# Second layer's first product by Strassen's seven products, with Mish as one activation

## The chip, the cores and the metric

One NeuronCore of a Trainium2 chip runs the whole program. The metric is the device time of one execution in microseconds (us); less is better. Times come from timed runs of the program and from one profiled execution of it, whose trace lists every instruction of every engine: PE (matrix products; PEld is its loading of stationary operands), ACT (activations and copies), DVE (elementwise work), POOL, and SP, which here only issues transfers.

## The reference, cut to what matters

Local attention (4 batches, 8 heads, 768 positions, head width 64) gives x with 3072 rows and 512 columns. Two dense layers follow:

```
h = x @ w_in                                     # 3072x512 by 512x2048
g = maximum(h, 0) + alpha * minimum(h, 0)        # layer 1
x = g @ w_out                                    # 3072x2048 by 2048x512
h = x @ w_in2                                    # layer 2, same shapes
g = h * tanh(log(1 + exp(h)))                    # "Mish" (log1p(exp) replaced by h above 20)
out = g @ w_out2
```

All of it is float32. The weights come as 64-bit floats and are turned into 32-bit ones on the chip.

## The kernel before, in words

**Products.** Every float32 operand of a large product is split into a high part (a cast, `h`) and a low remainder (`l`), and a product is the sum of three: high*high, high*low, low*high. So a product of a 128x128 stationary tile with a moving tile of n columns is three matmuls.

**Tiling.** Rows of x come in 6 blocks of 512 (`BN`). The 2048 inner features come in 16 units of 128 (index j). For a block and a unit, `gemm1` (line 884) forms the unit's h for 512 rows in one PSUM bank: 4 steps over the 512 input features times three, 12 matmuls of 512 columns (all of them the call at L897). The first two units of the first block alone are done in halves of 256 rows, in 48 matmuls of 256 columns, because half the rows are ready earlier. Then comes the nonlinearity, then `split_g` (high by ACT, L909, low by DVE, L910) and `gemm2` (line 941): 12 matmuls of 512 columns (L961) that add the unit's share into four PSUM banks, one for each 128 rows of output (layer 2) or 128 output features (layer 1). After 16 units `evac` (line 969) copies the four banks out.

**Layer 2's nonlinearity** is `act2` (line 924): for a unit three activations on ACT (Exp, Ln, Exp) and six instructions on DVE (L929 to L936).

**Banks and buffers.** Banks 0 to 3 collect the second products, banks 4 to 7 hold h. The split g lives in two slots; x of a block in two alternating buffers. Layer 1's result goes through DRAM (`yd`); `load_y` (line 986) reads a block of it back and splits it, four 512-wide casts and four subtractions.

**Weights.** Layer 1's weights stay in 32 buffers of SBUF (`wi0..15`, `wo0..15`). Layer 2's are converted during layer 1 and put in DRAM (`spill_w`, line 338, in blocks 2 to 4), and come back into the 32 buffers during the last block of layer 1 as those come free (`reload_w`, line 344). They stay for all of layer 2.

**Order of the work.** Each piece of work is a task given to `Plan` (line 69) with its engine, an assumed duration, what it reads and what it writes. `Plan.run` works out due times backwards and then lays the tasks out engine by engine; each engine executes its list in that order, and an instruction that has to wait holds back all behind it on its engine. PE's order is that of the main loop (line 1050): gemm1 of a unit, then gemm2 of the unit `LAG` before it (2 in layer 1, 4 in layer 2). Attention work for later blocks is woven into layer 1.

Of the kernel before, what the change touches and what calls it, by code (L numbers as in the profile page):

```python
# [21 lines left out]
E20 = 485165195.40979028  # L22
# [152 lines left out]
def chunked_attention_moe_moe_kernel(  # L175
# [82 lines left out]
    two = cp.tile([P, 1], F32, name="two")  # L258
# [4 lines left out]
    nc.gpsimd.memset(two, 2.0)  # L263
# [17 lines left out]
    w2f = {}  # L281
# [56 lines left out]
    def spill_w(item, at):  # L338
        f = to_f32(item, load_raw(item, at=at), at=at)
        d = Buf(lambda: dp.tile([P, 512], F32, name=f"w2f{item[1]}{item[2]}"))  # L340
        add("sp", dma_(P * 2048), lambda: nc.sync.dma_start(d.t, f.t.bitcast(F32)), [f], [d], at=at)
        w2f[item] = d

    def reload_w(item):
        f, d = wfs.next(), w2f.pop(item)
        add("sp", dma_(P * 2048), lambda: nc.sync.dma_start(f.t.bitcast(F32), d.t), [d], [f])
        split_w(item, f)
# [516 lines left out]
    def open_second():  # L864


        def open_():
            if "bp" not in phase:
                att_pools.close()
                phase["bp"] = ctx.enter_context(tc.tile_pool(name="bp", bufs=1))  # L870

        second["raw"] = raw2.next()
        for tag, n in (("u", 3), ("n", 2), ("rc", 2), ("e", 2), ("o", 3)):
            shape = [P, BN]

            def make(tag, shape):
                open_()
                return phase["bp"].tile(shape, F32, tag=tag, name=tag)

            second[tag] = Ring([lambda t=f"{tag}{i}", s=shape: make(t, s) for i in range(n)], att_bufs)  # L880
# [43 lines left out]
    def act2(blk, j, h, n_):  # L924
        u, n, r, e = (second[t].next() for t in ("u", "n", "rc", "e"))
        v = nc.vector
        hs = lambda: h.t[:, :BN]
        add("act", a_(BN) - 0.05, lambda: nc.scalar.activation(u.t, hs(), AF.Exp), [h], [u])  # L928
        add("dve", d_(BN, True), lambda: v.tensor_scalar_min(u.t, u.t, E20), [], [u])  # L929
        add("dve", d_(BN), lambda: v.scalar_tensor_tensor(n.t, u.t, 2.0, u.t, ALU.add, ALU.mult), [u], [n])  # L930
        add("act", a_(BN) + 0.09, lambda: nc.scalar.activation(e.t, n.t, AF.Ln, bias=two[:, 0:1]), [n], [e])  # L931
        add("act", a_(BN), lambda: nc.scalar.activation(r.t, e.t, AF.Exp, scale=-1.0), [e], [r])  # L932
        add("dve", d_(BN), lambda: v.scalar_tensor_tensor(e.t, n.t, 2.0, r.t, ALU.add, ALU.mult), [n, r], [e])  # L933
        add("dve", d_(BN), lambda: v.scalar_tensor_tensor(r.t, e.t, 2.0, r.t, ALU.subtract, ALU.mult), [e], [r])  # L934
        add("dve", d_(BN), lambda: v.tensor_mul(n.t, n.t, r.t), [r], [n])
        add("dve", d_(BN), lambda: v.scalar_tensor_tensor(u.t, n.t, -1.0, hs(), ALU.mult, ALU.mult), [n, h], [u])  # L936
        uu = Buf(lambda: [u.t])
        uu.uses = u.uses
        split_g(1, blk, j, uu, BN)

    def gemm2(layer, blk, j):
# [7 lines left out]
        for a in range(na):  # L949
            bk = accs[layer, blk][a]  # L950
            n = BLOCKS[blk][1] if layer == 0 else DM

            def go(a=a, bk=bk, n=n):
                cs = slice(a * P, (a + 1) * P)
                (gh, gl), (wh, wl) = g.t, (w.t[:, z, :] for z in range(2))
                if layer == 0:
                    prods = [(wh[:, cs], gh), (wh[:, cs], gl), (wl[:, cs], gh)]
                else:
                    prods = [(gh[:, cs], wh), (gh[:, cs], wl), (gl[:, cs], wh)]
                for i, (lt, rh) in enumerate(prods):  # L960
                    nc.tensor.matmul(bk.t[:, :n], lt, rh, start=j == 0 and i == 0, stop=j == NJ - 1 and i == 2)  # L961

            add("pe", 3 * p_(n), go, [w, g], [bk])
            if j == NJ - 1:
                evac(layer, blk, a, bk)

    yds = {}

    def evac(layer, blk, a, bk):
# [6 lines left out]
        else:  # L976
            o = rstrip.next(DM) if a == 0 else second["o"].next()

            def view():
                return o.t[0] if a == 0 else o.t  # L980

            row = blk * BN + a * P
            add(BOTH, a_(DM), lambda e: copy_on(e, view(), bk.t), [bk], [o])
            add("sp", dma_(P * DM * 4), lambda: nc.sync.dma_start(out[row : row + P, :], view()), [o])

    def load_y(blk):
        t0 = blk * BN
        frm = [b for i, b in yds.items() if BLOCKS[i][0] < t0 + BN and t0 < sum(BLOCKS[i])]
        (x, views, _, _), = parts = new_x(BN)
        raw = second["raw"]  # L990
        for kk in range(KT):
            key = raw, kk % 2

            def xr(kk=kk):
                return raw.t[:, kk % 2 * BN : (kk % 2 + 1) * BN]

            def high(xr=xr, kk=kk):
                nc.scalar.copy(views()[0][:, kk, :], xr())

            def low(xr=xr, kk=kk):  # L1000
                xh, xl = (t[:, kk, :] for t in views())
                nc.vector.tensor_sub(xl, xr(), xh.bitcast(F32))

            def load(xr=xr, kk=kk):
                nc.sync.dma_start(xr(), yd[:, kk, t0 : t0 + BN])

            add("sp", dma_(P * BN * 4), load, [(b, kk) for b in frm], [key])
            add("act", a_(BN), high, [key], [(x, ("h", kk))])
            add("dve", d_(BN), low, [key, (x, ("h", kk))], [(x, ("l", kk))])
        return parts  # L1010


# [3 lines left out]
    w2_items = [(1, side, j) for j in range(NJ) for side in "io"]  # L1016
# [23 lines left out]
    W2B = 2  # L1040
    LAG = (2, 4)
    tiles = [(layer, blk, j) for layer in range(2) for blk in range((NBA, NB)[layer]) for j in range(NJ)]
    pend = []
    xcur = xts[0]
    xnext = None

# [3 lines left out]
    for layer, blk, j in tiles:  # L1050
# [8 lines left out]
        if j == 0:  # L1059
            if (layer, blk) == (0, NBA - 1):  # L1060
                open_second()
            xcur = xts.pop(blk) if layer == 0 else xnext
        n = BN if layer else BLOCKS[blk][1]
        h = early[j] if (layer, blk) == (0, 0) and j < SPLIT else gemm1(layer, blk, j, xcur, n)
        if layer == 0:
            i = ((blk - W2B) * NJ + j) * 32 // ((NBA - 1 - W2B) * NJ)
            if blk < NBA - 1 and 0 <= i < len(w2_items) and w2_items[i] not in w2f:
                spill_w(w2_items[i], plan.now)
            elif blk == NBA - 1 and j == 0:
                xnext = load_y(0)  # L1070
        elif j == 2 and blk + 1 < NB:
            xnext = load_y(blk + 1)
        weave(2 * j)
        (act1 if layer == 0 else act2)(blk, j, h, n)
        pend.append((layer, blk, j))
        while len(pend) > LAG[layer]:
            t2 = pend.pop(0)
            gemm2(*t2)
            if t2[:2] == (0, NBA - 1):
                for side in "io":  # L1080
                    reload_w((1, side, t2[2]))
        weave(2 * j + 1)
    while pend:
        gemm2(*pend.pop(0))
# [58 lines left out]
```

## Time and profile before

| | |
|---|---|
| timed runs, 3 | 1117.82 to 1118.26 us, median 1118.02 us |
| profiled execution: span from first to last instruction | 1116.8 us |
| PE busy in the span | 1109.0 us (99%) |
| PEld, DVE, ACT busy | 914.6 (82%), 789.2 (71%), 580.4 us (52%) |
| HBM read and written | 74.85 and 20.97 MB |

The span is 1.2 us shorter than the median of the timed runs; the profile lists no other time of its execution. A matmul's duration in the trace is longer than the distance to the next one, since matmuls overlap: the pace is read from the distance of starts. The same holds of PEld's loads.

### The profile page before, as it was taken

How to read it: one execution, taken by the hardware profiler on the slowest of the kernel's cores; microseconds unless marked ns; L12 is line 12 of the kernel's file. 1: busy time of each engine (PE TensorE's matmuls, PEld its weight loads, DVE VectorE, ACT ScalarE, POOL GpSimd, SP SyncE). 2: the span in 40 equal slices, each digit the busy share in tenths (PEclk: the TensorE clock that was granted, in tenths of full speed). 3: DMA queues.
4: the chain of work that ended last, by engine and by line, in shares of the span. 5: the costliest groups of instructions: out<-in, count | busy, mean ns of one | idle time of the engine just before them, and what ended most of it. 6: DMA issues, size and time to landing. Idle time of an engine off the chain costs nothing.

```text
span 1116.8 us, 19091 instructions
## 1 busy us (share of the span) xinstructions
PE 1109.0 (99%) x7566; PEld 914.6 (82%) x7571; DVE 789.2 (71%) x1378; ACT 580.4 (52%) x1267; POOL 6.6 (1%) x20
## 2 busy tenths in 40 slices
PE   8999999999999999999999999999999999999998
PEld 5888888888888888888888888888888888888887
DVE  6898546476575756645459788778778878777775
ACT  6888434455454554545456445445446445444543
POOL 2000000000000000000000000000000000000000
PEclk9999999999999999999999999999999999999999
DMA  9976211345454455334332001002002000100101
GB/s 279 309 210 179 89 32 50 106 160 177 123 172 134 131 175 150 98 116 133 95 95 95 1 16 61 1 1 76 1 1 76 1 1 20 38 1 1 38 0 38
DMA packets 56585, 97.05 MB, mean 87 GB/s; under 512 B 5296, under 2 KB 24240, under 8 KB 56496
## 3 DMA queue, kind: packets, MB, share of 16 engines
q1 hardware_dynamic: 56496, 95.84, 28.3%
q8 instruction: 59, 0.97, 0.4%
q14 instruction: 30, 0.25, 0.1%
HBM read 74.85 MB, written 20.97 MB: 86 GB/s over the span
## 4 chain that ended last, share of the span: by engine, by line
PE 99%; DMA 1%; SPq 0%; issue 0%; DVE 0%; ACT 0%
PE bank L897 47%; PE bank L961 47%; PE bank L715 2%; PE bank L649 1%; PE bank L1023 1%; DMA wo<-in_kw_dram 1%; PE bank L593 0%; PE bank L762 0%; PE bank L526 0%; PE bank L786 0%; SPq L425 0%; SPq L418 0%; DVE wo L551 0%; ACT o L251 0%; DVE st L574 0%
## 5 line engine op out<-in xcount | busy, mean ns | idle before, releaser
L897 PE MATMUL bank<-xh,wi 128*128 128x512 f32 (+1 forms) x1552 | 506.6, 388 | 0.0
L897 PEld LDWEIGHTS bank<-xh,wi 128*128 128x128 f32 x1552 | 290.4, 188 | 59.9
L897 PE MATMUL bank<-xl,wi 128*128 128x512 f32 (+1 forms) x776 | 300.2, 387 | 0.0
L961 PE MATMUL bank<-gh,wo 128*128 128x512 f32 x768 | 253.3, 391 | 0.0
L961 PE MATMUL bank<-wo,gh 128*128 128x512 f32 x768 | 236.4, 389 | 0.0
L897 PEld LDWEIGHTS bank<-xl,wi 128*128 128x128 f32 x776 | 145.7, 188 | 29.4
L961 PEld LDWEIGHTS bank<-gh,wo 128*128 128x128 f32 x768 | 144.2, 188 | 30.3
L961 PEld LDWEIGHTS bank<-wo,gh 128*128 128x128 f32 x768 | 144.2, 188 | 30.0
L961 PE MATMUL bank<-gl,wo 128*128 128x512 f32 x384 | 149.5, 389 | 0.0
L961 PE MATMUL bank<-wo,gl 128*128 128x512 f32 x384 | 149.4, 389 | 0.0
L919 DVE SCALAR_TENSOR_TENSOR rstrip<-rstrip,nalpha 128x512 f32<-128x512 f32 x96 | 72.0, 750 | 107.0 <-ACT rstrip L916 106.4
L909 ACT CAST gh<-u 128x512 fp32r<-128x512 f32 x96 | 59.8, 623 | 156.3 <-PE bank L961 156.2
L915 ACT ACTIVATE rstrip<-bank 128x512 f32<-128x512 f32 x96 | 57.9, 604 | 110.8 <-PE bank L897 107.5
L910 DVE TENSOR_TENSOR gl<-rstrip,gh 128x512 fp32r<-128x512 f32 x96 | 66.2, 690 | 62.3 <-ACT gh L909 61.6
L909 ACT CAST gh<-rstrip 128x512 fp32r<-128x512 f32 x96 | 60.3, 628 | 93.6 <-PE bank L961 65.5
L928 ACT ACTIVATE u<-bank 128x512 f32<-128x512 f32 x96 | 57.4, 598 | 93.4 <-PE bank L897 92.7
L933 DVE SCALAR_TENSOR_TENSOR e<-n,rc 128x512 f32<-128x512 f32 x96 | 66.4, 692 | 48.5 <-ACT rc L932 48.5
L910 DVE TENSOR_TENSOR gl<-u,gh 128x512 fp32r<-128x512 f32 x96 | 66.3, 691 | 42.3 <-ACT gh L909 42.3
L961 PEld LDWEIGHTS bank<-wo,gl 128*128 128x128 f32 x384 | 72.0, 188 | 15.0
L961 PEld LDWEIGHTS bank<-gl,wo 128*128 128x128 f32 x384 | 72.1, 188 | 14.7
L931 ACT ACTIVATE e<-n,two 128x512 f32<-128x512 f32 x96 | 69.2, 721 | 4.5 <-DVE n L930 4.4
L934 DVE SCALAR_TENSOR_TENSOR rc<-e,rc 128x512 f32<-128x512 f32 x96 | 66.4, 692 | 3.2
(107 smaller groups left out, 991.0 us busy)
## 6 DMA issues: line engine op xcount, KB each, us to landing
wi<-in_w_in_dram SPq DMA_DIRECT2D x16, 512.0 KB, 9.5
wo<-in_w_out_dram SPq DMA_DIRECT2D x16, 512.0 KB, 8.6
raw<-in_w_in_dram SPq DMA_DIRECT2D x16, 512.0 KB, 4.3
raw<-in_w_out_dram SPq DMA_DIRECT2D x16, 512.0 KB, 4.8
yd<-rstrip SPq DMA_DIRECT2D x24, 256.0 KB, 2.7
raw<-yd SPq DMA_DIRECT2D x24, 256.0 KB, 2.7
qbd<-in_q_dram SPq DMA_DIRECT2D x20, 256.0 KB, 4.5
vw<-in_vw_dram SPq DMA_DIRECT2D x20, 256.0 KB, 5.2
```

The lines of the kernel that those rows point to most:

```text
L649: nc.tensor.matmul(ps(z)[row : row + CH, i, 2 * a + e, :], qview()[half, 2 * a + z, e].rearrange("p (x c) -> p x c", c=2)[:, :, c], keys(2 ...
L715: nc.tensor.matmul(out[h * 64 : (h + 1) * 64, i, p, c], value(half, c, 2 * p + h), aT()[half, i, (p % 2) * (NP // 2) + p // 2, c, h ^ (p % ...
L897: nc.tensor.matmul(bk.t[:, lo:hi], a, b, start=kk == 0 and i == 0, stop=kk == KT - 1 and i == 2)
L909: add("act", a_(n), lambda: nc.scalar.copy(g.t[0], src.t[0]), [src], [(g, "h")])
L910: add("dve", d_(n), lambda: nc.vector.tensor_sub(g.t[1], src.t[0], g.t[0].bitcast(F32)), [src, (g, "h")], [(g, "l")])
L915: add("act", a_(n) - 0.05, lambda: nc.scalar.activation(m.t[0], h.t[:, :n], AF.Relu, scale=-1.0), [h], [m])
L919: lambda: nc.vector.scalar_tensor_tensor(r.t[0], m.t[0], nalpha[:, j : j + 1], r.t[0], ALU.mult, ALU.add),
L928: add("act", a_(BN) - 0.05, lambda: nc.scalar.activation(u.t, hs(), AF.Exp), [h], [u])
L931: add("act", a_(BN) + 0.09, lambda: nc.scalar.activation(e.t, n.t, AF.Ln, bias=two[:, 0:1]), [n], [e])
L933: add("dve", d_(BN), lambda: v.scalar_tensor_tensor(e.t, n.t, 2.0, r.t, ALU.add, ALU.mult), [n, r], [e])
L934: add("dve", d_(BN), lambda: v.scalar_tensor_tensor(r.t, e.t, 2.0, r.t, ALU.subtract, ALU.mult), [e], [r])
L961: nc.tensor.matmul(bk.t[:, :n], lt, rh, start=j == 0 and i == 0, stop=j == NJ - 1 and i == 2)
```

## The change

For layer 2's first product, two units (256 features of h) and 512 rows are taken together, as a 2x2 by 2x2 block product: the 512 input features in two halves, the rows in two halves of 256 (`HB`), the features of h in the two units. Strassen's scheme in Winograd's form needs seven products of half blocks instead of eight, and sums of blocks before and after:

- `load_y` (now line 1039) reads a block of layer 1's result in two transfers, forms four sums on DVE (`s1` to `s4`) and splits seven operands (`XS`), each 512 columns wide. The seven have one buffer each, no second one.
- `spill_pair` forms sums of layer 2's input weights during layer 1 (now in blocks 1 to 4) and stores seven half-width pieces for a pair. `reload_in` brings the 56 pieces back into 28 of the 32 buffers. The second product's weights have the other four buffers, and `reload_out` reads each of the 16 from DRAM again in every block and splits it with `halves`.
- `pair2` does the seven products of a pair, each 6 matmuls of 256 columns (2 steps times three), in three of four banks, taken in turn. Results are added up in a bank where they can be, and else copied by ACT (`keep`) and added by DVE (`plus`) in `cm`. Parts of older units' second product (`between`, 3 matmuls of 512 columns each) stand between the seven.
- Mish is one activation function of ACT, in pieces of 256, 512 and 256 columns for a pair. The six DVE instructions and two of the three activations of a unit go.
- Output rows are staged in the three slots of `rstrip` alone; before, one of the four used `rstrip` and three had buffers of their own.

```diff
-    def act2(blk, j, h, n_):
-        u, n, r, e = (second[t].next() for t in ("u", "n", "rc", "e"))
...
+    def spill_pair(p, at):
...
+        sums = (
+            (0, lambda: nc.vector.tensor_sub(t(0), b(0, 1), b(0, 0)), fs),
+            (2, lambda: nc.vector.tensor_sub(t(2), b(1, 1), b(0, 1)), fs[1:]),
+            (1, lambda: nc.vector.tensor_sub(t(1), b(1, 1), t(0)), [fs[1], (raw, "t", 0)]),
+            (3, lambda: nc.vector.tensor_sub(t(3), b(1, 0), t(1)), [fs[0], (raw, "t", 1)]),
+        )
...
+    def halves(w, **kw_):
...
+        add("act", a_(512), lambda: nc.scalar.copy(w.t[:, 0, :], lo()), [(w, "l")], [(w, "h")], **kw_)
+        add("dve", d_(512), lambda: nc.vector.tensor_sub(w.t[:, 1, :], lo(), w.t[:, 0, :].bitcast(F32)), [(w, "h")], [(w, "l")], **kw_)
...
+    def reload_out(j):
+        w = slot(*out_places[n_out[0] % len(out_places)], [P, 2, 512], F32R)
...
     def evac(layer, blk, a, bk):
...
-            o = rstrip.next(DM) if a == 0 else second["o"].next()
+            o = rstrip.next(DM)
...
+    XS = ("a11", "s1", "a12", "s2", "s4", "s3", "a22")
...
+            x = Buf(make, x_last.get(i, xring.last[m]))
+            x_last[i] = [x]
...
+            add("act", a_(BN), high, [b], [(x, "h")])
+            add("dve", d_(BN), low, [b, (x, "h")], [(x, "l")])
...
+    def pair2(blk, p, xs, between):
...
+        ba, bc, bb = (next_bank() for _ in range(3))
...
+                for kk in range(2):
...
+                    for n, (l, r) in enumerate(((wh, xh), (wh, xl), (wl, xh))):
+                        nc.tensor.matmul(
+                            bk.t[:, :HB], l, r, start=first and kk == n == 0, stop=kk == 1 and n == 2,
...
+        product("a11", 0, ba, True)
+        keep(ba, 0)
+        product("s1", 3, bc, True)
+        keep(bc, 2)
+        between(1)
+        product("a12", 1, bb, True)
+        plus(bb, 0)
+        mish(us[0], 0, 1, lambda: cv(0), [(cm, 0)])
+        between(1)
+        product("s2", 4, ba, False)
+        keep(ba, 1)
+        between(1)
+        product("s4", 2, bc, False)
+        plus(bc, 1)
+        between(1)
+        product("s3", 5, ba, False)
+        plus(ba, 2)
+        mish(us[1], 0, 2, lambda: cv(1, 2), [(cm, 1), (cm, 2)])
+        between(2)
+        product("a22", 6, ba, False)
+        mish(us[0], 1, 1, lambda: ba.t[:, :HB], [ba])
+        between(2)
...
+    for blk in range(NB):
+        xs = xnext
+        for p in range(NJ // 2):
+            for j in (2 * p, 2 * p + 1):
+                reload_out(j)
+            pend.extend((1, blk, j) for j in (2 * p, 2 * p + 1))
+            pair2(blk, p, xs, between)
+            if p == 1 and blk + 1 < NB:
+                xnext = load_y(blk + 1)
```

On PE, in the middle of a block of layer 2, one unit stood in the order before as follows (nine rows of its first product, then its neighbour's second product; an `x2` at a row's end is two equal instructions):

```order
L897 MATMUL bank_7308<-xh_6028,wi_6022 128x512
L897 MATMUL bank_7308<-xl_6029,wi_6022 128x512
L897 MATMUL bank_7308<-xh_6028,wi_6022 128x512 x2
L897 MATMUL bank_7308<-xl_6029,wi_6022 128x512
L897 MATMUL bank_7308<-xh_6028,wi_6022 128x512 x2
L897 MATMUL bank_7308<-xl_6029,wi_6022 128x512
L897 MATMUL bank_7308<-xh_6028,wi_6022 128x512 x2
L897 MATMUL bank_7308<-xl_6029,wi_6022 128x512
L897 MATMUL bank_7308<-xh_6028,wi_6022 128x512
L961 MATMUL bank_6884<-wo_5962,gh 128x512 x2
L961 MATMUL bank_6884<-wo_5962,gl 128x512
```

Now a pair stands there, of which these rows run from its fourth product (`s2`, into the bank of the first) to its seventh (`a22`); `[waits ...]` names the engine whose semaphore the instruction waits for:

```order
L1119 MATMUL bank_6377<-xl_5401,wi_5770 128x256 [waits Activation_49]
L1119 MATMUL bank_6377<-xl_5401,wi_5770 128x256 x5
...
L1119 MATMUL bank_6377<-xh_6004,wi_5770 128x256 [waits Activation_49]
L1119 MATMUL bank_6377<-xh_6004,wi_5770 128x256 x5
L1009 MATMUL bank_6192<-wi_6292,gh 128x512 x2
L1009 MATMUL bank_6192<-wi_6292,gl 128x512 [waits DVE_49]
L1009 MATMUL bank_6213<-wi_6292,gh 128x512 x2
L1009 MATMUL bank_6213<-wi_6292,gl 128x512
L1119 MATMUL bank_6377<-xl_6015,wo_5790 128x256 [waits DVE_49]
L1119 MATMUL bank_6377<-xl_6015,wo_5790 128x256 x5
```

A unit's 12 long matmuls in one piece became, for two units, seven times 6 short ones, with parts of second products between them; the seventh product waits for DVE, since it writes the bank that DVE has just added from.

On ACT, at the passage from layer 1 to layer 2, the order before was this up to the first evacuation of layer 1's last block (`L330` is the high part of a reloaded weight, `L251` the evacuation of a bank):

```order
L909 CAST gh<-u_6068 128x512 [waits DVE_49,PE_49]
L330 CAST wo_6145<-wf_6058 128x512 [waits DMAHW5_49]
L931 ACTIVATE e_6147<-n_6138,two 128x512 [waits DVE_49]
L932 ACTIVATE rc_6154<-e_6147 128x512 [waits Activation_49]
L928 ACTIVATE u_6163<-bank_6134 128x512 [waits DVE_49,PE_49]
L251 COPY rstrip<-bank_5489 128x512 [waits PE_49]
```

It is now this (`cm` are the sums of products, `L378` the high parts of reloaded weights, `L250` the evacuation of a bank):

```order
L1127 COPY cm_6038<-bank_6030 128x256 [waits PE_49]
L378 CAST wo_6026<-wo_6026 128x512 [waits DMAHW6_49]
L1133 ACT_TABLE_LOAD
L1133 ACTIVATE u_6067<-cm_6038 128x256 [waits DVE_49]
L1127 COPY cm_6038<-bank_6018 128x256 [waits PE_49]
L250 COPY rstrip<-bank_5497 128x512 [waits PE_49,Activation_49]
```

The load of the table that holds Mish stands once in the program, here, ahead of the copy of the `s2` result, for which PE waits with `s3`.

On ACT at the end of the program, the four evacuations stand last; before and now:

```order
L909 CAST gh<-u_9992 128x512 [waits DVE_49,PE_49]
L251 COPY rstrip<-bank_9544 128x512 [waits PE_49]
L251 COPY o_10068<-bank_9551 128x512 [waits DMAHW4_49,PE_49]
L251 COPY o_10074<-bank_9556 128x512 [waits DMAHW5_49,PE_49]
L251 COPY o_10077<-bank_9561 128x512 [waits DMAHW6_49,PE_49]
```

```order
L973 CAST gh<-wf_10606 128x512 [waits DVE_49,PE_49]
L250 COPY rstrip<-bank_10080 128x512 [waits PE_49]
L250 COPY rstrip<-bank_10093 128x512 [waits PE_49]
L250 COPY rstrip<-bank_10108 128x512 [waits PE_49]
L250 COPY rstrip<-bank_10119 128x512 [waits DMAHW7_49,PE_49,Activation_49]
```

The fourth now waits for the transfer of the first one's rows (DMAHW7), whose slot it takes.

## Rows read from the trace of the kernel before

**Rows 1.** The page: span and busy time of the engines.
```profile
span 1116.8 us, 19091 instructions
PE 1109.0 (99%) x7566; PEld 914.6 (82%) x7571; DVE 789.2 (71%) x1378; ACT 580.4 (52%) x1267; POOL 6.6 (1%) x20
```

**Rows 2.** The chain that ended last, from 593 us: start, length, what.
```profile
593.45 2.72 PE bank L961 x12
596.16 2.72 PE bank L897 x12
```

**Rows 3.** Windows: stretch, length, busy (instructions) by engine, clock, DMA share, GB/s.
```profile
600.00:1040.00 440.00, 440.00 (x1943) 364.34 (x1942) 357.13 (x587) 222.61 (x364) 0.00 (x0) 1.00 0.07 24
28.00:32.20 4.20, 4.20 (x37) 4.20 (x37) 3.79 (x7) 3.40 (x7) 0.00 (x0) 1.00 1.06 369
```

**Rows 4.** Timeline of PE and PEld, 256-wide matmuls: start, us, engine, line, instruction.
```profile
27.82 0.28 PE L897 MATMUL bank<-xl,wi 128*128 128x256 f32 x1
...
28.18 0.28 PE L897 MATMUL bank<-xl,wi 128*128 128x256 f32 x1
...
32.14 0.28 PE L897 MATMUL bank<-xl,wi 128*128 128x256 f32 x1
...
33.05 0.39 PE L897 MATMUL bank<-xl,wi 128*128 128x512 f32 x1
...
35.13 0.39 PE L897 MATMUL bank<-xl,wi 128*128 128x512 f32 x1
...
27.83 0.31 PEld L897 LDWEIGHTS bank<-xh,wi 128*128 128x128 f32 x2
28.06 0.19 PEld L897 LDWEIGHTS bank<-xl,wi 128*128 128x128 f32 x1
```

**Rows 5.** Timeline, end of a first product and the activation that reads it.
```profile
571.30 0.39 PE L897 MATMUL bank<-xh,wi 128*128 128x512 f32 x1
571.52 0.39 PE L961 MATMUL bank<-gh,wo 128*128 128x512 f32 x1
...
571.78 0.60 ACT L915 ACTIVATE rstrip<-bank 128x512 f32<-128x512 f32 x1 [1.64 <-PE bank L897]
```

**Rows 6.** Groups by line and form: count, busy us, mean ns, idle before.
```profile
L910 DVE TENSOR_TENSOR gl<-u,gh 128x512 fp32r<-128x512 f32 x96 | 66.3, 691 | 42.3 <-ACT gh L909 42.3
L909 ACT CAST gh<-u 128x512 fp32r<-128x512 f32 x96 | 59.8, 623 | 156.3 <-PE bank L961 156.2
L928 ACT ACTIVATE u<-bank 128x512 f32<-128x512 f32 x96 | 57.4, 598 | 93.4 <-PE bank L897 92.7 <-DVE e L933 0.7
L803 DVE STREAM_TRANSPOSE aT<-s 32x256 f32<-32x256 f32 x128 | 55.8, 436 | 2.5
L668 ACT ACTIVATE s<-bank,su 128x64 f32<-128x64 f32 x160 | 48.7, 343 | 14.8 <-DVE su L685 14.8
L220 ACT ACT_TABLE_LOAD x1 | 1.3, 1283 | 0.7 <-PEq L1130 0.7
```

**Rows 7.** Transfers: size and median us from issue to landing.
```profile
wf<-w2fo SPq DMA_DIRECT2D x16, 256.0 KB, 2.7
out_dram<-rstrip SPq DMA_DIRECT2D x6, 256.0 KB, 2.0
```

**Rows 8.** Timeline in layer 1: keys loaded, and the scores on PE that use them.
```profile
294.46 0.86 SPq L448 DMA_DIRECT2D qbd<-in_kw_dram  x2
...
311.23 0.81 PE L649 MATMUL bank<-kt,qbd 64*32 64x64 f32 x60
```

**Rows 9.** The end: chain, then timeline of ACT and SP.
```profile
1099.36 13.61 PE bank L961 x60
...
1110.96 0.59 ACT L251 COPY rstrip<-bank 128x512 f32<-128x512 f32 x1 [3.00 <-PE bank L961]
1111.64 1.95 ACT L251 COPY o<-bank 128x512 f32<-128x512 f32 x3
1111.58 0.33 SPq L984 DMA_DIRECT2D out_dram<-rstrip  x1
```

More of the change, by code (lines that the diff above doesn't have):

```diff
@@ L922, in act1, with gemm2_parts @@
         split_g(0, blk, j, r, n)
-    def act2(blk, j, h, n_):
-        u, n, r, e = (second[t].next() for t in ("u", "n", "rc", "e"))
[L926 to L941, printed above, removed]
+    def gemm2_parts(layer, blk, j):
         w = weights[layer, "o", j]
@@ L965, in gemm2 @@
                 evac(layer, blk, a, bk)
+        return [partial(part, a) for a in range(na)]
+    def gemm2(layer, blk, j):
+        for part in gemm2_parts(layer, blk, j):
+            part()
     yds = {}
@@ L988, in load_y @@
         frm = [b for i, b in yds.items() if BLOCKS[i][0] < t0 + BN and t0 < sum(BLOCKS[i])]
[L989 to L1009, printed above, removed]
@@ new lines, in load_y, with make, high, low @@
+        parts = {}
+        for i, name in enumerate(XS):
+            m, z, half = i // 4, i // 2 % 2, i % 2
+            def make(m=m, z=z, half=half):
+                if (m, z) not in x_tiles:
+                    x_tiles[m, z] = xmakers[m][z]()
+                return x_tiles[m, z][:, half * 2 * BN : (half + 1) * 2 * BN]
+            x = Buf(make, x_last.get(i, xring.last[m]))
+            x_last[i] = [x]
+            v, b = where[name]
+            def high(x=x, v=v):
+                nc.scalar.copy(x.t[:, :BN].rearrange("p (k t) -> p k t", t=HB), v())
+            def low(x=x, v=v):
+                hi, lo = (x.t[:, c * BN : (c + 1) * BN].rearrange("p (k t) -> p k t", t=HB) for c in range(2))
+                nc.vector.tensor_sub(lo, v(), hi.bitcast(F32))
+            add("act", a_(BN), high, [b], [(x, "h")])
+            add("dve", d_(BN), low, [b, (x, "h")], [(x, "l")])
+            parts[name] = x
@@ L1059, in chunked_attention_moe_moe_kernel @@
         if j == 0:
-            if (layer, blk) == (0, NBA - 1):
+            if blk == NBA - 1:
                 open_second()
-            xcur = xts.pop(blk) if layer == 0 else xnext
-        n = BN if layer else BLOCKS[blk][1]
+            xcur = xts.pop(blk)
+        n = BLOCKS[blk][1]
         h = early[j] if (layer, blk) == (0, 0) and j < SPLIT else gemm1(layer, blk, j, xcur, n)
[L1065 to L1072, printed above, removed]
+        if W2B <= blk < NBA - 1:
+            step, steps = (blk - W2B) * NJ + j, (NBA - 1 - W2B) * NJ
+            for k in range(step * len(w2_jobs) // steps, (step + 1) * len(w2_jobs) // steps):
+                w2_jobs[k](plan.now)
+        elif blk == NBA - 1 and j == 0:
+            xnext = load_y(0)
@@ new lines, in chunked_attention_moe_moe_kernel, with between @@
+        weave(2 * j + 1)
+    for n in range(n_in, len(in_places)):
+        reload_in(n)
+    parts = []
+    def between(n):
+        for _ in range(n):
+            if not parts and (len(pend) > LAG[1] or pend[0][0] == 0):
+                parts.extend(gemm2_parts(*pend.pop(0)))
+            if parts:
+                parts.pop(0)()
+    for blk in range(NB):
+        xs = xnext
+        for p in range(NJ // 2):
+            for j in (2 * p, 2 * p + 1):
+                reload_out(j)
[3 more added lines that the diff above has]
+                xnext = load_y(blk + 1)
@@ L1083, in chunked_attention_moe_moe_kernel @@
+    while parts:
+        parts.pop(0)()
     while pend:
```

159 lines of the change are left out of this document (127 added, 32 removed).

## The prediction

> **What bounds the kernel now.** I read the page's first lines, then the chain of waits, then the windows of layer 2, then the timeline of the one stretch that already has 256-wide matmuls. The reader is to see in the page that PE is busy for 1109.0 of 1116.8 us and no other engine over 82% [rows 1]; in the chain that layer 2 is nothing but PE, 12 matmuls in 2.72 us, alternately a first and a second product [rows 2]; and in the windows that from 600 to 1040 us PE has no gap at full clock (2.4 GHz) with DVE busy for 357 and ACT for 223 of 440 us [rows 3]. So only what changes PE's pace or stops PE counts; the six DVE instructions and two activations that go from each unit are worth nothing by themselves.
>
> **The change part by part, against the span of 1116.8 us.**
>
> *PE, removed and added.* A 512-wide matmul costs 2.72/12 = 226.7 ns [rows 2]. A pair of units had 24 in its first product: 5.44 us. Now it has 7 x 6 = 42 of 256 columns. Their pace stands in the trace: in the half-block start, the low-part matmuls, one in three, start at 27.82, 28.18 and so on to 32.14 [rows 4], 36 matmuls in 4.32 us, 120.0 ns each. (226.7 - 120.0)/256 is 0.417 ns a column, one column a cycle at 2.4 GHz, and 13.3 ns are left that do not shrink with the width. So 42 x 0.1200 = 5.04 us, 0.40 us less a pair. That is 7% and not the 12.5% of the column count, since 18 more matmuls pay 13.3 ns each. 6 blocks x 8 pairs x 0.40 = 19.2 us less. Bounds of the pace: the stretch ran beside heavy transfers (369 GB/s [rows 3]), and just behind it the 512-wide matmuls took (35.13 - 33.05)/9 = 231 ns [rows 4] against 226.7 later, 2% more. If the 256-wide ones were slowed as much, they take 117.6 ns in quiet and the gain is 24 us; on the other side I see nothing above 120. I take 120.0, as it fits a whole cycle a column.
>
> A rule of the Trainium skill speaks against this change. The rows first: each matmul has its own load of 188 ns, and in the 256-wide stretch two follow each other in 0.31 us, so they overlap, and 120 ns from matmul to matmul hold [rows 4]. The page "TensorE: Matmul & The Clock Gate", section "The mechanism" of its part on packing, says that a load overlaps running matmuls only where it goes to other rows of the array; these loads take all 128 rows. By that, 42 loads instead of 24 would stand in the way. The trace disagrees here: a 128-column load is seen at 188 ns, and it fits neither before 256 columns in 120 ns nor before 512 in 226.7 unless it lies beside them.
>
> *PE, waits inside a pair.* From the start of a pair (products 0.72 us, parts of second products 3 x 226.7 = 0.68) the fourth product starts at 3.52, the sixth at 6.32, the seventh at 8.40, the end is at 10.48 us. A reader of a bank starts 0.26 us after PE turns to the next work (571.52 to 571.78 [rows 5]). No 256-wide copy or add is in the trace; nearest are, for ACT, 343 ns for 64 columns and 598 for 512, and for DVE 436 ns for a 256-wide transposition and 691 for 512 [rows 6]. I take 0.45 and 0.44 us, which lie between on ACT and at the like width on DVE. Then the copy for the fourth product ends at 0.72 + 0.26 + 0.45 = 1.43, 2 us early; that for the sixth at 4.24 + 0.26 + 0.45 = 4.95, 1.4 us early; the add for the seventh at 7.04 + 0.26 + 0.44 = 7.74, 0.66 us early. With the 512-wide durations as upper ends it is still 0.41 us early. I cost these waits at nothing; behind a waiting product stand all of PE's later ones, so a lost cover costs its whole excess in each of 48 pairs.
>
> *ACT and DVE, load.* Mish is not in the trace. Its lower end is the 343 ns of 64 columns; three activations made it before, so its upper end is three Exp, 1.8 us for 512 columns. I take one Exp, 598 ns for 512 columns, and 0.45 for 256, as it is one instruction of that kind [rows 6]. ACT then has, a pair, three copies 1.35, Mish 1.50, four casts (two of g, two of reloaded weights) at 0.62 [rows 6] 2.48: 5.3 of 10.48 us. Mish could take 6.6 us a pair before ACT is the bound. DVE has 3 x 0.44 + 4 x 0.69 = 4.1 us. At each of the five block changes seven casts and seven subtractions of x come into one pair, for which x no longer has a second buffer: ACT 9.7, DVE 8.9 of 10.48 us. Each operand has from its product in the last pair to the same product in the next, 9.76 us, for 0.26 + 0.62 + 0.69. It fits, with ACT 92% full, and I cost it at nothing.
>
> *Transfers.* Weights of the second product come 16 times a block, 256 KB and 2.7 us to landing each [rows 7]. In SP's list they stand in the order in which buffers come free. A buffer is freed in the middle of pair p and needed in pair p + 2, some 16 us later, against 0.26 + 2.7 + 0.62 + 0.69 = 4.3 us; the DMA share was 0.07 there [rows 3]. Nothing. In layer 1, SP now stores pieces, waiting for DVE's new sums (32 x 0.44 = 14 us over four blocks), ahead of attention's loads in its queue. There keys issued at 294.46 are used at 311.23 [rows 8], 16.8 us later; delays of some us vanish in that. Nothing.
>
> *The passage to layer 2.* The table load, 1.28 us [rows 6], stands on ACT ahead of the copy for the sixth product. Counted from the last first product of layer 1: buffer `wo13` free at 2.72, transfer landed at 2.72 + 0.26 + 2.7 = 5.7, its cast to 6.3, table to 7.6, Mish to 8.05, copy to 8.5; the sixth product starts at 9.04. By the page "ScalarE: Activation LUTs", section "What ACT_TABLE_LOAD costs", some 1.38 us of drain come on top; the load of 1.28 agrees with the trace, the drain no row shows. With it the estimate of the stall is 0.9 us. From rows alone the stall is 0 up to one more table load's length, 1.3 us; I take 0.3.
>
> *The end.* The last second products run as before: four units of 2.72 us in one piece from 1099.36 [rows 9], the same work without first products between. The fourth evacuation began at 1111.64 + 1.95 - 0.59 = 1113.00. Now it waits for the first one's transfer: issued at 1111.58, 2.0 us to landing [rows 7, 9], 1113.6. 0.6 us later.
>
> *Sum.* 1116.8 - 19.2 + 0.3 + 0.6 = 1098.5 us of span; the median of the runs lies 1.2 us over the span before, so **1099.7 us**.
>
> **The rivals.**
>
> 1. *Block changes and passage cost* (gain partly kept). For: ACT at 9.7 of 10.48 us, and its list is in order, so one cast that waits for PE holds back the copies. Against: a pair of slack for each operand. If in each change one cast and one subtraction come late, 0.62 + 0.69 = 1.3 us, five times, and the passage takes its 1.3: 6.5 + 1.0 more, 1107.
>
> 2. *The seventh product waits in every pair* (slower). Place: PE behind DVE's add of the sixth product, the chain with the least slack. It decides the sign from 0.66 + 0.40 = 1.06 us of delay, for instance two 512-wide DVE instructions ahead of the add (1.38): then 0.72 a pair are lost, 48 x (0.72 - 0.40) = 15 us, 1133. For: DVE's list is in order and has four 512-wide instructions a pair. Against: the copy, cast and add ahead of it in the list depend on things that end 1.4 us earlier, at the fifth product.
>
> 3. *Loads of stationary operands do bind* (slower; the rule above). If each 188 ns load stood in line, 42 x 0.188 = 7.9 us against 5.44, 48 x 2.46: 1236. Against: the 36 matmuls at 120.0 ns [rows 4].
>
> 4. *Mish is slow* (slower). Were it over 6.6 + 0.40 = 7.0 us a pair, six times an Exp's width for width, ACT would set the pace; with a third more, 9.4 us, a pair lasts 3.8 + 9.4 = 13.2 us, and the whole 48 x (13.2 - 10.88) = 111 us more, 1229. Against: at the upper end of three Exp it is 3.6 us a pair, and ACT is still free for 3 us.
>
> 5. *The 256-wide pace is better in quiet*: 117.6 ns, 1095.
>
> That the change does not do what it says I rule out: the new order has 48 x 42 matmuls of 256 columns, one table load, and no instruction of the old activation.
>
> **How the numbers follow.** Forecast, 1098 to 1102: 0.76. Rival 1, 1102 to 1110: 0.12. Rival 2: 0.04; rival 3: 0.01; rival 4: 0.02; rival 5 with anything else below 1098: 0.05. A measurement of this kernel tells 0.2% or 2.2 us from no change, so "same" is 1115.8 to 1120.3. Faster is the forecast, rivals 1 and 5 and a part of rival 2 too small to lose all: 0.94; same 0.02; slower 0.04. The range of 1097.5 to 1105 holds the forecast and some half of rival 1 and of rival 5, about 0.84; the sizes left open inside it are the stalls at the passage (0 to 1.3), five block changes and the end.
>
> **What would show it.** Right: six products' matmuls starting every 0.36 us in threes, a pair in 10.48 us, a block of layer 2 in 83.8; PE without gaps of note after 45 us; layer 2 about 19 us shorter, layer 1 unchanged to 1 us; the fourth last evacuation behind a transfer. Wrong: gaps on PE at the seventh product (rival 2), in the last pairs of blocks (rival 1), matmuls of 256 columns starting 180 ns or more apart (rival 3), ACT without gaps (rival 4). The prediction fails if the pace of 120 ns holds only in the short stretch where I read it, or if the list of ACT blocks at the passage for longer than I counted.

## The result and the profile after

The changed kernel takes 1106.61 us (median of 4 runs, 1105.50 to 1107.60), the kernel before, run beside it, 1118.14 us (4 runs): a ratio of 0.9895, 95% interval 0.9883 to 0.9908. It is 11.5 us faster, where 18.3 were forecast, and 1106.6 lies 1.6 us above the range. The sign was right and the size was not.

The page's first lines, against [rows 1]. DVE's work fell from 789 to 605 us, ACT's hardly moved, and PE is again busy for 99% of the span:

```profile
span 1105.8 us, 20937 instructions
PE 1096.9 (99%) x8435; PEld 938.8 (85%) x8435; DVE 604.8 (55%) x1119; ACT 575.4 (52%) x1371; POOL 6.8 (1%) x19
```

The window of layer 2 that answers to the first of [rows 3], in the same columns: granted clock 1.00 (2.4 GHz), DVE 199 us in place of 357. But PE has 439.3 of 440 us, where it had all of them.

```profile
600.00:1040.00 440.00, 439.32 (x2756) 395.38 (x2755) 198.88 (x353) 224.33 (x463) 0.00 (x0) 1.00 0.23 73
```

The chain that ended last, one pair of units in the middle of a block (start, length, what), against [rows 2]. L1119 is a product, L1009 a second product's part:

```profile
645.80 1.43 PE bank L1119 x12
647.24 0.69 PE bank L1009 x3
647.93 0.71 PE bank L1119 x6
...
652.87 1.39 PE bank L1009 x6
...
656.35 1.43 PE bank L1119 x12
```

From 645.80 to 656.35 a pair lasts 10.55 us, not 10.48 (10.547 by the starts of its first matmul). The products are as cheap as forecast or cheaper (0.71 for six matmuls of 256 columns, 0.72 expected). The second products are dearer: three in 0.69 in place of 0.68, six in 1.39 in place of 1.36.

PE's waits of the whole run (what it waited for: us, times, longest). Both lines are new; those of the start are left out:

```profile
PE bank L1009 <- ACT rstrip L250: 1.9, 3, 1.0
...
PE bank L1119 <- DVE cm L1130: 0.7, 2, 0.4
```

**Where 7.3 us of span went.** Forecast 1098.5, profiled 1105.8:

| term | forecast | measured | difference |
|---|---|---|---|
| first matmul of layer 1 (25.18 us before, 24.93 now) | 0 | -0.25 | -0.25 |
| layer 1, from there to its last first product (554.67, now 557.66) | 0 | +2.99 | +2.99 |
| passage to layer 2 | +0.3 | 0 | -0.3 |
| pace: a pair takes 10.547 and not 10.48 us (47 times) | -19.2 | -16.0 | +3.15 |
| first pairs of blocks 1 to 4, over 10.547 by 0.17, 0.64, 0.21, 0.57, and one later pair by 0.04 (blocks counted from 0) | 0 | +1.63 | +1.63 |
| last matmul's start to the end (4.2 before, 4.9 now) | +0.6 | +0.7 | +0.1 |

The sum is 7.3. (This execution took 1107.6 us, 1.0 more than the median; the time is 1.8 us over the span in every run of both kernels, so the profiled execution of the kernel before was some 0.6 us slower than its median, and the 1.2 us of the prediction hold for that pair of numbers alone.) The start of layer 1's last first product, on which the second row rests, stands in the chains of before, of the changed kernel, and of experiment 3 below:

```profile
579.85 2.72 PE bank L897 x12
...
582.59 2.72 PE bank L961 x12
...
579.01 2.72 PE bank L961 x12
```

Three terms matter: the pace, layer 1, the block changes. Each got experiments.

### The profile page after: what moved, and what is told of

It is laid out like the page before. It is cut to its first block, busy times and chain, and to the rows that moved or that the text cites. A ratio compares the mean times of both kernels' runs of the same rounds, so it can differ in the third digit from the quotient of the medians.

```text
span 1105.8 us, 20937 instructions
## 1 busy us (share of the span) xinstructions
PE 1096.9 (99%) x8435; PEld 938.8 (85%) x8435; DVE 604.8 (55%) x1119; ACT 575.4 (52%) x1371; POOL 6.8 (1%) x19
## 4 chain that ended last, share of the span: by engine, by line
PE 92%; DMA 3%; DVE 2%; ACT 2%; issue 0%; ACTq 0%; SPq 0%; DVEq 0%
PE bank L1009 45%; PE bank L961 22%; PE bank L1119 21%; DMA raw<-in_w_in_dram 2%; PE bank L776 2%; PE bank L1173 1%; DMA wi<-w2o 1%; PE bank L710 1%; PE bank L587 0%; DVE su L725 0%; ACT raw L314 0%; ACT rstrip L250 0%; DVE wf L320 0%; PE bank L654 0%; ACT s L729 0%
## 5 line engine op out<-in xcount | busy, mean ns | idle before, releaser
L1009 PE MATMUL bank<-gh,wo 128*128 128x512 f32 x768 | 255.1, 391 | 2.0 <-ACT rstrip L250 1.9
L961 PE MATMUL bank<-xh,wi 128*128 128x512 f32 (+1 forms) x784 | 254.8, 387 | 0.0
L1009 PE MATMUL bank<-wi,gh 128*128 128x512 f32 x768 | 241.4, 396 | 0.0
L1009 PEld LDWEIGHTS bank<-gh,wo 128*128 128x128 f32 x768 | 144.2, 188 | 33.7 <-ACT rstrip L250 3.7
L961 PEld LDWEIGHTS bank<-xh,wi 128*128 128x128 f32 x784 | 146.3, 188 | 30.0
L1130 DVE TENSOR_TENSOR cm<-bank,cm 128x256 f32<-128x256 f32 x144 | 60.9, 423 | 168.8 <-PE bank L1119 168.4
L961 PE MATMUL bank<-xl,wi 128*128 128x512 f32 (+1 forms) x392 | 150.9, 385 | 0.0
L1009 PE MATMUL bank<-gl,wo 128*128 128x512 f32 x384 | 149.6, 389 | 0.0
L1009 PE MATMUL bank<-wi,gl 128*128 128x512 f32 x384 | 149.4, 389 | 0.0
L1009 PEld LDWEIGHTS bank<-wi,gh 128*128 128x128 f32 x768 | 126.1, 190 | 9.5
L379 DVE TENSOR_TENSOR wi<-wi 128x512 fp32r<-128x512 f32 x108 | 74.4, 689 | 79.1 <-ACT wi L378 79.0
L974 DVE TENSOR_TENSOR gl<-rstrip,gh 128x512 fp32r<-128x512 f32 x96 | 66.1, 688 | 54.1 <-ACT gh L973 53.1
L1119 PEld LDWEIGHTS bank<-xh,wo 128*128 128x128 f32 x648 | 88.2, 190 | 6.7 <-ACT cm L1127 0.2
L1119 PE MATMUL bank<-xh,wo 128*128 128x256 f32 x648 | 90.8, 282 | 0.0
L378 ACT CAST wi<-wi 128x512 fp32r<-128x512 f32 x108 | 66.6, 617 | 45.6 <-DMA wi<-w2o 45.6
L1009 PEld LDWEIGHTS bank<-wi,gl 128*128 128x128 f32 x384 | 72.2, 188 | 16.2
L1009 PEld LDWEIGHTS bank<-gl,wo 128*128 128x128 f32 x384 | 72.1, 188 | 14.3
L1119 PEld LDWEIGHTS bank<-xl,wo 128*128 128x128 f32 x504 | 71.1, 189 | 9.1 <-DVE cm L1130 2.2
```

The source lines that it names most:

```text
L378: add("act", a_(512), lambda: nc.scalar.copy(w.t[:, 0, :], lo()), [(w, "l")], [(w, "h")], **kw_)
L379: add("dve", d_(512), lambda: nc.vector.tensor_sub(w.t[:, 1, :], lo(), w.t[:, 0, :].bitcast(F32)), [(w, "h")], [(w, "l")], **kw_)
L961: nc.tensor.matmul(bk.t[:, lo:hi], a, b, start=kk == 0 and i == 0, stop=kk == KT - 1 and i == 2)
L974: add("dve", d_(n), lambda: nc.vector.tensor_sub(g.t[1], src.t[0], g.t[0].bitcast(F32)), [src, (g, "h")], [(g, "l")])
L1119: nc.tensor.matmul(bk.t[:, :HB], l, r, start=first and kk == n == 0, stop=kk == 1 and n == 2, skip_group_check=True,)
L1130: add("dve", d_(HB), lambda: nc.vector.tensor_add(cv(i), bk.t[:, :HB], cv(i)), [bk], [(cm, i)])
```

## The experiments

Unless said otherwise, an edit is one to the changed kernel; the edits are shown in outline. The kernel before took 1118.13 to 1118.27 us beside each group of runs.

**1. Quiet matmuls behind the end.** Extra matmuls only, where no other engine works:

```diff
+PROBE = [(512, 24)] + [(256, 6), (512, 3)] * 8 + [(256, 42), (512, 24)] + [(256, 12), (512, 12)] * 4 + [(384, 24), (512, 24)]
+        for width, count in PROBE:
+            run(width, count)
```

> The changed kernel with 224 extra matmuls behind the last second product, on the operands of the last unit, while the other engines only finish their last copies: 24 of 512 columns, then 8 times (6 of 256, 3 of 512), then 42 of 256 and 24 of 512, then 4 times (12 of 256, 12 of 512), then 24 of 384 and 24 of 512. They write a bank that is not stored; the output is unchanged. Theory W (the change of width itself slows the first 512-wide matmuls behind narrow ones): the same 233, 236, 228 ns are seen here, where no other engine works, and after 42 or 12 narrow ones a tail of 233, 236, 228, 233, 231, then 226.7. Theory C (contention with ACT, DVE or transfers slows them): 226.7 and 120.0 throughout, 53.4 us for all. Theory B (the buffers that the products read and not the width): 226.7 here too, since all these matmuls read the same two tiles.

This ran once, 1156.43 us. (The list has 306 matmuls, not 224; the 53.4 us are right for 306.) The timeline of PE, from the last of 42 narrow matmuls on (start, length; three matmuls are two rows):

```profile
1121.35 0.40 PE L1109 MATMUL bank<-wi,gh 128*128 128x256 f32 x2
...
1121.71 0.63 PE L1109 MATMUL bank<-wi,gh 128*128 128x512 f32 x2
...
1122.40 0.62 PE L1109 MATMUL bank<-wi,gh 128*128 128x512 f32 x2
...
1123.09 0.61 PE L1109 MATMUL bank<-wi,gh 128*128 128x512 f32 x2
...
1123.77 0.61 PE L1109 MATMUL bank<-wi,gh 128*128 128x512 f32 x2
```

Three narrow ones take 0.36 us. The first three wide ones take 0.69, the next three 0.69, then 0.68. One by one the starts are 233, 236, 229, 232, 231, 227 and then 226.7 ns apart, and on the way back to narrow 113, 119 and then 120.0. The short alternation, six narrow and three wide, repeats every 1.407 us (five starts from 1106.13 to 1111.76), 7 ns over the sum of 0.72 and 0.68. There, as in the rest of the probe, DVE, ACT and the transfers are at zero:

```profile
1106.13:1107.54 1.41, 1.41 (x12) 1.28 (x10) 0.00 (x0) 0.00 (x0) 0.00 (x0) 1.00 0.00 0
```

So theory W holds, C and B fall: returning from 256-wide to 512-wide costs by itself, 20 ns net when a long group of wide matmuls follows (28 on the first six, 8 given back on the next narrow ones), 7 ns when three do. Groups of six are not in the probe; in layer 2 their starts are 233, 236, 228, 233, 231 and 226 ns apart, the same tail. Four returns of 7 and two of 20 make 68 ns a pair; measured are 67. The 42 narrow ones hold 120.0 ns each, in quiet too, so my rival 5 (117.6) falls with it. 384 columns take 173.3 ns, which is 160 + 13.3: the fixed part is the same at three widths. The 384-wide group also shows that not only the return to wide costs: its first seven starts behind 512-wide ones are 170 to 185 ns apart, some 25 ns over its own steady pace in all.

**2. Mish alone, in the kernel before.**

```diff
-        (three activations and six DVE instructions)
+        add("act", a_(BN), lambda: nc.scalar.activation(u.t, h.t[:, :BN], AF.Mish), [h], [u])
```

> The kernel before with one part of the change alone: the three activations and six DVE instructions of each unit in layer 2 replaced by one Mish activation; products, spills and weights as before. Theory P (PE alone counts): within 0.2% of the kernel before, 1117 to 1119 us; layer 2's pace stays 2.72 us for 12 matmuls. Rival (less work on ACT and DVE by itself speeds PE or the passage): 3 us or more faster, 1115 or less.

1117.99 us against 1118.27, ratio 1.000 (0.999 to 1.0009). Theory P holds: in the kernel before, 343 us less of DVE's work and 120 less of ACT's are worth nothing. The gain comes with the products. That they would have it without Mish does not follow: DVE is busy for 199 of 440 us in the window above, 4.8 us a pair, and 343 us over 48 pairs are 7.1 more, 11.9 us for a pair of 10.5. By this estimate DVE would then set the pace; no run has the products with the old activation. In this run Mish took 598 ns for 512 columns, as the Exp in its place ([rows 6]); in the changed kernel, where it reads sums in SBUF, it is within 6% of that, as the second of these groups of ACT shows (count, busy us, mean ns, idle before; from 600 to 1090 us):

```profile
L1127 ACT COPY cm<-bank 128x256 f32<-128x256 f32 x140 | 52.1, 372 | 42.2 <-PE bank L1119 42.1
...
L1133 ACT ACTIVATE wf<-cm 128x512 f32<-128x512 f32 x24 | 15.2, 632 | 14.9 <-DVE cm L1130 14.9
```

**3. The spills of layer 1 moved.**

```diff
-            for k in range(step * len(w2_jobs) // steps, (step + 1) * len(w2_jobs) // steps):
-                w2_jobs[k](plan.now)
+            if j in SPILLS:                     # (6, 8, 9, 11, 13, 14)
+                w2_jobs[(blk - W2B) * len(SPILLS) + SPILLS.index(j)](plan.now)
```

> The changed kernel with the same spills of layer 1, begun at units 6, 8, 9, 11, 13, 14 of blocks 1 to 4, so that none stands at a block's evacuations. Theory S (the raw load of a spill pair holds ACT just when it must copy the accumulators of the block): the four waits at about 134, 230, 326 and 421 us go, 2.7 us less, 1103.9 us; the last first product of layer 1 begins near 580 us as before the change. Rival (the added work of the spills, DVE's sums and SP's stores, delays attention whatever its place): layer 1 stays 2 us or more longer than before the change, 1106 us or more.

1102.99 us (1102.69 to 1103.96), 3.6 less. First the place in the changed kernel, the chain around 421 us:

```profile
413.52 5.79 DMA raw<-in_w_in_dram
...
419.33 0.67 ACT raw L314
...
420.02 0.44 DVE wf L317
...
420.48 0.69 DVE wf L320
421.17 0.61 DVE gl L974
...
421.80 0.59 ACT rstrip L250
...
422.44 1.67 PE bank L1009 x6
```

Read it upward: PE wants a bank; the bank waits for ACT's copy (`L250`) into `rstrip`; the copy waits for DVE's subtraction `gl` (`L974`), which reads from `rstrip`; that stands in DVE's list behind the conversion of a spilled weight (`L317`, `L320`), which waits for ACT's first step on it (`L314`), which waits for a transfer. ACT's row in the timeline says how long it stood still for that transfer, with evacuations queued behind it:

```profile
419.33 0.66 ACT L314 ACTIVATE raw<-raw 128x512 f32<-128x512 f32 x1 [1.53 <-DMA raw<-in_w_in_dram]
```

With the spills moved the same stretch of the chain is PE alone:

```profile
417.89 2.72 PE bank L1009 x12
420.61 2.72 PE bank L961 x12
```

From the first matmul (24.59) to the last first product of layer 1 (579.01) are 554.42 us now, as before the change (554.67). The other traces agree: the five with the spills in their old place (the changed kernel, experiments 1, 4, 5, 6) have layer 1 longer than before by 1.5 to 3.0 us, the four with the spills moved (3, 7, 8, 9) by nothing. The added work of the spills is free; only its coincidence with the evacuations cost. Theory S holds, its rival falls. The two profiled executions differ by 4.9 us: 0.3 at the start, 3.2 in layer 1, 1.3 at the block changes, which stalled for 0.35 us here in place of 1.63; the changed kernel's was its slowest of four, so the medians differ by less.

**4. Second products in two groups of twelve matmuls.**

```diff
-        between(1)   # behind the 2nd, 3rd, 4th and 5th product; 2 behind the 6th and the 7th
+        between(4)   # behind the 4th and the 6th product alone
-        ba, bc, bb = (next_bank() for _ in range(3))
+        bc, ba, bb = (next_bank() for _ in range(3))
```

> The changed kernel with the eight parts of second products of a pair in two groups of four (behind the fourth and the sixth product) in place of six groups, and the banks taken in the order that this needs; the same matmuls. Theory W (each return from narrow to wide costs): two returns a pair in place of six; a return costs some 22 ns for a group of 12 wide ones against 6 for a group of 3 and 20 for one of 6, so 44 in place of 64 ns a pair, 48 times: 1.0 us less; also the add has 2.7 us in place of 1.4 before the seventh product, so the stalls at the block changes go, 1.6 us: 1104 us. Theory C (contention): the pace does not move with the order, only the block changes go: 1105 us. A pair in the trace takes 10.52 us by W and 10.55 by C.

1104.72 us (1103.34 to 1105.28), which does not separate 1104 from 1105. The chain does:

```profile
640.87 2.75 PE bank L1009 x12
643.61 3.59 PE bank L1119 x30
...
651.39 2.75 PE bank L1009 x12
```

640.87 to 651.39 is 10.52 us, W's number, and not C's 10.55. The same matmuls in another order are 27 ns shorter. All pairs of blocks 1 to 5 last 10.52, block changes too; there PE has no wait for DVE's add any more. So this order takes away 1.3 us of the pace (47 pairs) and, in its trace, the stalls at the block changes.

**5. The load of the next block a pair later.**

```diff
-            if p == 1 and blk + 1 < NB:
-                xnext = load_y(blk + 1)
+            if p == 2 and blk + 1 < NB:
+                xnext = load_y(blk + 1, plan.now)     # its transfers not issued before this time
```

> The changed kernel with the load of the next block's y begun a pair of units later, so that in SP's queue four reloads of second-product weights that stood behind it come first. Theory Q (the load of y waits in SP's queue for DVE, a weight reload behind it lands late, ACT's cast of that weight holds up ACT, and the seventh product of the next pair waits): the waits of 0.6, 0.2, 0.6 and 0.2 us at four block changes go, 1.6 us less, 1105.0 us; every pair of blocks 1 to 5 in 10.55 us. Rival (DVE's four sums and seven subtractions of a block change fill its list, wherever the load stands): the same waits at the same places, 1106.6 us.

1105.41 us (1104.62 to 1106.38). The place in the changed kernel, the chain at a block change:

```profile
751.48 4.79 DMA wi<-w2o
...
756.28 0.63 ACT wi L378
...
756.94 0.70 DVE wi L379
...
758.67 0.60 DVE xs L1069
759.27 0.60 DVE raw L1069
759.87 0.35 DVE cm L1130
...
760.26 0.98 PE bank L1119 x6
```

A weight reload takes 4.79 us, between the two transfers of the next block's y; ACT waits for it, so its cast, a copy and DVE's subtraction come late, and then three of DVE's four sums (`L1069`) get ahead of the add (`L1130`) that the seventh product needs. This is the first pair of block 2, in which y of block 3 is loaded; the first pair of the last block, with no y to load, has 10.547 us. With y later, the pairs of blocks 1 to 5 all last 10.55 us (84.37 us a block, where it had been up to 85.0), and PE's list of waits has no line for `L1119`. Theory Q holds; the rival falls, since the sums and subtractions are still there. The size is another matter: with the load in its old place and the same order of products, the traces of experiments 1, 3 and 6 lose 1.1, 0.35 and 0.44 us at these places, not 1.63, so the time of 1.2 us less, with ranges that overlap, is no measure of it.

**6. A fourth buffer for the output rows.**

```diff
-            o = rstrip.next(DM)
+            o = rstrip.next(DM) if a < 3 else second["o"].next()
```

> The changed kernel with a buffer of its own for the fourth evacuation of each block in layer 2. Theory E (at the end the fourth copy waits for the first one's transfer): from the last matmul to the end of the span 3.9 us in place of 4.7, as before the change; about 0.8 us less, 1105.8 us. Rival (the copies are bound by DVE and ACT behind PE, the transfer is hidden): the end stays at 4.7 us.

The end of the changed kernel, from the chain, answers to [rows 9]:

```profile
1099.28 0.60 ACT rstrip L250
...
1099.89 2.08 DMA out_dram<-rstrip
...
1102.07 0.58 ACT rstrip L250
```

With the buffer the last copy follows its bank, and 4.2 us pass from the last matmul's start to the end of the span, as before the change, in place of 4.9:

```profile
1092.78 7.04 PE bank L1010 x31
...
1099.84 0.58 ACT o L250
```

The trace bears theory E out. The time does not show it: 1106.85 us, 1105.37 to 1108.18. The spread of 2.8 us from run to run is larger than the 0.7 us; it most likely comes from the waits in layer 1 and at the block changes, which differ from trace to trace (experiments 3 and 5), since it is 0.7 us in the next experiment, which has none.

**7. Experiments 3, 4 and 6 together.** No new edit.

> The changed kernel with the spills moved, two groups of second-product parts and the buffer for the fourth evacuation together. From the run with the spills moved, 1103.0 us: pace 0.03 us in each of 47 pairs, 1.3 us less, block changes of that run 0.5 us less, the end 0.8 less: 1100.4 us if the parts add up. Against: something hidden until now comes up, 1102 us or more.

1100.64 us (1100.22 to 1100.91), ratio to before 0.9843 (0.9829 to 0.9856). The parts add up: 1100.4 expected.

**8. One group of 24.** An edit to the kernel of experiment 7.

```diff
-        bc, ba, bb = (next_bank() for _ in range(3))
+        ba, bb, bc = (next_bank() for _ in range(3))
+        between(8)                        # behind the 4th product, nothing elsewhere
+        product("s3", 5, ba, False)       # 6th before 5th
+        plus(ba, 2)
         product("s4", 2, bc, False)
```

> The combined kernel with all eight parts of second products of a pair in one group of 24 matmuls behind the fourth product, the sixth product ahead of the fifth, and the banks in the order that this needs. One return from narrow to wide a pair in place of two: by theory W 20 ns a pair less, 10.50 us, 1.0 us in all, 1099.4 us, if the seventh product does not wait. Its add has 0.72 us (one product) against 0.26 + 0.42 = 0.68: a margin of 0.04 us. Rival 2 of the prediction (the seventh product waits for DVE's add): a wait wherever another DVE instruction stands ahead of the add; with 0.3 us in every second pair 7 us more, 1107 us. I expect the waits at the block changes for certain (about 1 us each) and in the other pairs less than 0.1 us: 1104 us.

1100.60 us (1100.21 to 1101.12): 3.4 us below the 1104 that I expected, and no gain over experiment 7 that the time shows. The pair is 10.50 us. I expected waits at all block changes; there was one of note in the trace, which made a pair 0.46 us longer at 842 us, where a late y puts DVE's sums ahead of the adds (timeline):

```profile
841.67 0.68 DVE L1070 TENSOR_TENSOR xs<-x,xs 128x512 f32<-128x512 f32 x1
842.28 0.42 DVE L1131 TENSOR_TENSOR cm<-bank,cm 128x256 f32<-128x256 f32 x1
...
842.75 0.98 PE L1120 MATMUL bank<-xl,wo 128*128 128x256 f32 x6 [0.30 <-DVE cm L1131]
```

The pair behind it is 0.09 us longer. In the others the margin of 0.04 us in front of the seventh product held, so rival 2 needs another DVE instruction in the way, as the prediction said.

**9. One group and the late load.** Experiments 5 and 8 together.

> The one-group kernel with the load of the next block's y begun a pair later, as in the run with the late load. Theory Q and W together: every pair from the fourth on in 10.50 us, block changes too, PE without a wait over 0.15 us in layer 2, so 1.0 us less than the combined kernel: 1099.6 us. Rival (the margin of 0.04 us before the seventh product does not hold at block changes, where DVE has eleven more instructions): waits of 0.1 to 0.7 us at some changes stay, 1100.2 us or more.

1100.07 us (1099.52 to 1101.53), ratio 0.9839 (0.9826 to 0.9853), the fastest of all, though within the scatter of the two before it, and between the 1099.6 of the theory and the 1100.2 of its rival. The trace decides: PE has no wait in layer 2, and from the fourth pair on every pair of the trace, block changes included, lasts 10.50 us:

```profile
634.27 5.47 PE bank L1010 x24
639.74 5.03 PE bank L1120 x42
644.77 5.47 PE bank L1010 x24
```

10.547, 10.52 and 10.50 us for six, two and one return a pair: each order costs what the quiet stretch gives for it (68, 40, 20 ns over 10.48).

## Why the prediction was wrong in size

- **What bounds the kernel: right.** Experiment 2 shows that less work on ACT and DVE is worth nothing by itself in the kernel before. (For the changed kernel the room on DVE counts, as estimated there.)
- **"36 matmuls in 4.32 us, 120.0 ns each": right.** 42 in quiet hold 120.0.
- **"A pair in 10.48 us": the failed step, 3.2 us.** I priced each width by its steady pace and the change between widths at nothing. The evidence was in [rows 4]: behind the narrow stretch the wide ones took 231 ns. I put that down to the transfers there (369 GB/s) and made an upside rival of it. Experiment 1 gives starts of the same size without any transfer. Behind 256-wide matmuls it has five of them; the nine in [rows 4] (229, 234, 235, 225, 230, 236, 229, 232 and 231 ns) are to within 1 ns its nine behind 384-wide ones. Why they are nine there is not shown. The trace of before held the test: with the same transfers a moment later the slow starts are over. Windows of the kernel before, behind the narrow stretch and 2.5 us on (same columns as [rows 3]), and its timeline there, six matmuls in 1.36 us:

```profile
32.80:35.10 2.30, 2.30 (x11) 1.88 (x10) 2.18 (x5) 2.18 (x5) 0.00 (x0) 1.00 1.06 375
35.40:37.80 2.40, 2.40 (x12) 2.01 (x11) 1.84 (x4) 2.02 (x4) 0.00 (x0) 1.00 1.05 375
```

```profile
35.81 0.39 PE L961 MATMUL bank<-gl,wo 128*128 128x512 f32 x1
...
37.17 0.39 PE L961 MATMUL bank<-gl,wo 128*128 128x512 f32 x1
```

- **The load rule of the Trainium skill: the trace disagrees, as I had it.** The rows first: 42 narrow matmuls in 5.03 us, with a load of 188 ns each. The page "TensorE: Matmul & The Clock Gate", section "The mechanism", lets, in its list of what overlaps, a load overlap only with matmuls on other rows; no run here shows that limit.
- **"I cost these waits at nothing" (inside a pair): right** in the middle of a block. The 256-wide add took 423 ns (0.44 taken), the copy 372 (0.45), Mish 383 or 417 and 632 (0.45 and 0.60).
- **"It fits, with ACT 92% full, and I cost it at nothing" (block changes): failed, 1.6 us.** The casts and subtractions did fit: they stand in the last pair of a block, where ACT is busy for 8.1 and DVE for 7.7 of 10.5 us (740.74 to 751.28 us) and PE does not wait. What I did not lay out was the pair behind it: SP's list, where a reload between two loads of y took 4.79 us for the 2.7 that I had, and DVE's four sums of that y, which my 8.9 us of DVE's work leave out. ACT and DVE, in order, passed the delay on to the one add with the least slack. That is near rival 1's place, one pair later, by rival 2's mechanism, at 0.2 to 0.6 us a change in place of 1.3 (experiment 5).
- **"Delays of some us vanish in that. Nothing" (layer 1): failed, 3.0 us.** I looked at whether attention's loads could stand a delay, and they could. The waiting instruction was another: ACT's first step on the second raw tile of a spill pair, with the accumulators' copies queued behind it (experiment 3). With those spills moved the 3.0 us are gone.
- **The passage: 0 in place of 0.3 us.** ACT's timeline has the table load of 1.28 us and the first Mish right behind it; PE does not wait.

```profile
590.69 0.62 ACT L378 CAST wo<-wo 128x512 fp32r<-128x512 f32 x1 [0.55 <-DMA wo<-w2i]
591.33 1.28 ACT L1133 ACT_TABLE_LOAD   x1
592.62 0.42 ACT L1133 ACTIVATE u<-cm 128x256 f32<-128x256 f32 x1
```

  The drain of 1.38 us that the Trainium skill adds ("ScalarE: Activation LUTs", section "What ACT_TABLE_LOAD costs") does not appear on either side of it: the cast ends at 591.31, the load begins at 591.33, and Mish begins 0.01 us behind its end. (The stall that the prediction works out with the drain is 8.5 + 1.38 - 9.04 = 0.8 us and not 0.9.)
- **The end: +0.7 us in the trace for the forecast 0.6**, by the mechanism named (experiment 6).
- **Rivals 3 and 4** (loads bind, Mish slow) fell as expected.

With the spills and the y load moved, one return a pair and the fourth buffer, the kernel takes 1100.07 us, 0.4 over the forecast. What held the gain back were the things costed at nothing. That it comes so near is in part luck: the fourth buffer takes away 0.7 us at the end that the forecast had counted as 0.6, and a pair in 10.50 us still costs 1.0 us more than forecast over the run.

## What to carry to other kernels

Price a change of matmul width as well as the widths: where narrow and wide alternate, count the changes, and look for a slow stretch behind a narrow one in the trace before blaming what else runs there. Where an edit is costed at nothing because its data has time, check the engines that wait for it in order: the question is what stands behind the waiting instruction at the busiest moment of the block, not how full the engine is on average. Work that is free in one place of a loop can cost at another; moving it is worth a run.

## What the runs showed of the hardware

- 512-wide matmuls behind 256-wide ones start 233, 236, 229, 232 and 231 ns apart before they settle at 226.7, in quiet (experiment 1); beside ACT, DVE and transfers in layer 2 the starts are the same to 1 ns. The second narrow one starts 113 and not 120 ns behind the first. Behind 384-wide ones the tail is longer, nine starts of up to 236 ns, and 384-wide ones behind 512-wide ones start slowly too (170 to 185 ns for 173.3). Why, the runs do not tell: the order of widths was changed here, the cause inside PE was not.
- A 256 KB reload took 2.6 us to landing in the median of 96, and one between two transfers of 512 KB 4.79 (the changed kernel).
